# Batch 3's key and value loads issued at other places, and two masks of batch 1 moved, in a block-sparse attention and feed-forward kernel

## The chip, the cores and the metric

The kernel runs on one core of one Trainium2 chip. A core has TensorE (PE, matrix products, with its weight loads shown as PEld), VectorE (DVE), ScalarE (ACT), GpSimd (POOL) and SyncE (SP). POOL and SP also issue the DMAs here: POOL those that read the inputs (queue q0, "software_dynamic" in the profile), SP those between tiles, the transposing ones and the stores of the output (queue q1, "hardware_dynamic"). The metric is the device time of one execution in microseconds; the median of three runs counts.

## The reference, cut to what matters

Attention over 4 batches, 8 heads, 768 positions and 64 channels. A query sees the keys less than 16 positions away, and 24 block summaries: the maximum of the keys and the mean of the values of each block of 32. A feed-forward part follows, with x * sigmoid(1.702 x) between two products (512 to 2048 to 512).

```python
k_sum = k.reshape(B, H, nb, block, D).max(axis=3)
v_sum = v.reshape(B, H, nb, block, D).mean(axis=3)
scores_all = concat([where(|i - j| < 16, scale * q @ k.T, -1e9),
                     scale * q @ k_sum.T + log(block)], axis=-1)
a = softmax(scores_all)
x = a @ concat([v, v_sum])
h = x @ w_in
out = (h * sigmoid(1.702 * h)) @ w_out
```

## The kernel before, in words

The four batches run in a software pipeline: while batch b is in its feed-forward part, the attention of batch b+1 is done beside it. Every engine's instructions are recorded through the helper class `_Ordered`, which keeps the program order on each engine; so nearly every instruction in the profile carries that helper's line, L28, and the order written in the code is the order on the engine. Groups are told apart by their tiles.

One pass of the main loop, `for b in range(0, B - 1)`, has two parts. In the first, a loop over `n` in steps of 2, the first product of the feed-forward of batch b runs (tiles `ph`, 128x384, into `gT` by GELU), and beside it the keys and queries of batch b+1 are prepared. In the second, a loop over the 21 steps of `seq`, the second product runs (`product`, tiles poA, poB, poC), and `beside(b + 1, i)` puts small pieces of the attention of batch b+1 behind step i: the lists `plan1` (batch 1), `plan2` (batch 2) and `plan` (batch 3) say which. In them `sHP` is a group of scores with its exponential (half H, head pair P), `mHP` its mask (`a_sb` times `mk` on DVE), `vHG` the value product of two head pairs (`ps_av`) with its division on DVE (`rc`, `x`), `W0` to `W3` are the four copies of the block sums, `K`, `Q`, `V` issue loads, and `X` starts the transposing DMAs of the keys.

**Tiles.** `kxs[s]` and `qTs[s]` hold transposed keys and queries, `vw[s]` values, of batch b with s = b % 2. `kb` (two buffers) is where keys land before they are transposed by SP (`xk`); `qb` is the same for queries (`xq`). `rest_k(p, s, pool)` completes the keys of head pair p: DVE takes the maxima of the blocks (`ks<-kx`), POOL copies the halos (`kx<-kx`, three copies) and the block maxima (`kx<-ks`, one). For batch 2 it is called at n/2 = 3, 4, 5, 6 of the first part of b = 1, for pairs 0 to 3. The scores of pairs 0 and 1 follow at slot -1 of the second part, those of pairs 2 and 3 at slot 3.

**Block-sum rows.** `value_rows` sums the values of each block on PE (`ps_vs`); `sum_rows` copies the sums, in four groups of two heads, into partitions 0 to 31 of `vw[s]` (`vw<-vboth`; groups 0 and 2 on ACT, 1 and 3 on DVE in batch 2). Behind the last group `sum_dmas` has SP send all of these rows to partitions 64 to 95 of the other half of the tile (`vw<-vw`, 198 KB); the first value product `v00` at slot 10 needs them there.

**Loads of batch 3.** They are issued by POOL in `load_batch(3)`, called behind step 0 of the second part of b = 1. A gate, a copy of one element into `gate2` on POOL, makes POOL wait until the tile that it reads is written:

```python
if b == 3:
    pool.tensor_copy(out=gate2, in_=qTs[0][:, 0, 0:1])
load_turned(k, b, kb2, "kb")          # four loads of keys
if b == 3:
    pool.tensor_copy(out=gate2, in_=qTs[0][:, NP - 1, 0:1])
...
load_v(b)                             # four loads of values
```

The query loads of batch 3 come later, in `middle`, which is the first part of b = 2. At steps 10, 13, 15 and 16 of the second part of b = 1 sums of weights are made for `middle` by `win_sum`, on DVE and POOL (tiles `kx<-w_in_sb` and `qT<-w_in_sb`, in the storage of keys and queries that are done with).

Of the kernel before, what the change touches and what calls it, by code (L numbers as in the profile page):

```python
# [35 lines left out]
def kernel(  # L36
# [10 lines left out]
    B, H, S, D = q.shape  # L47
    block = 32
# [4 lines left out]
    NP = H // 2  # L53
    QT = 64
    NQ = S // QT
    NJ = S // 128
# [10 lines left out]
    pool = _Ordered(tc, nc.gpsimd)  # L67
# [13 lines left out]
    kb2, qb2 = {}, {}  # L81
# [26 lines left out]
    def load_turned(x, b, t2, name, gs_=(0, 1)):  # L108

        for g in gs_:  # L110
            t2[g] = castp2.tile([128, 2, NJ, 2, D], BF16, name=name, tag=name)
            for hh in range(2):
                h0 = hh * NP + 2 * g
                pool.dma_start(out=t2[g][:, :, :, hh].rearrange("p i a d -> p (i a) d"),
                               in_=x[b, h0:h0 + 2].rearrange("h (a p) d -> p (h a) d", p=128))

    def load_v(b):
        src = v[b].rearrange("h (j e p) d -> e p (h j) d", e=2, p=64)
        n = NJ * H // 2
        for i in range(2):  # L120
            for e in range(2):
                pool.dma_start(out=vw[b % 2][e * 64:e * 64 + 64, e].rearrange("p h j c -> p (h j) c")[:, i * n:i * n + n, 0:D],
                               in_=src[e, :, i * n:i * n + n])
# [71 lines left out]
    qTs = [keep.tile([128, NP, S], BF16, name=f"qT{s}") for s in range(2)]  # L195
    qT = [[qTs[s][:, p] for s in range(2)] for p in range(NP)]
    vw = [keep.tile([128, 2, H, NJ, VC], BF16, name=f"vw{s}") for s in range(2)]
# [39 lines left out]

    def load_batch(b):
        if b == 3:
            pool.tensor_copy(out=gate2, in_=qTs[0][:, 0, 0:1])  # L240
        load_turned(k, b, kb2, "kb")
        if b == 3:
            pool.tensor_copy(out=gate2, in_=qTs[0][:, NP - 1, 0:1])
        if b == 1:
            load_turned(q, b, qb2, "qb", (0,))
        load_v(b)
        if b < 3:
            load_turned(q, b, qb2, "qb", (1,) if b == 1 else (0, 1))
# [89 lines left out]
    def at(ap, start, dims):  # L338
        a = ap[:, start:start + 1]
        return bass.AP(tensor=a.tensor, offset=a.offset, ap=[a.ap[0]] + dims)  # L340

    def flat_kx(p, s):
        return kx[p][s].rearrange("p t c -> p (t c)")

    def key_rows(p, s, ks, eng=dve, j0=0):
        flat = flat_kx(p, s)
        n = NJ - j0
        eng.tensor_copy(out=at(flat, 256 * j0 + 64, [[256, n], [64, 2], [1, nb]]),
                        in_=ks.unsqueeze(1).unsqueeze(1).to_broadcast([128, n, 2, nb]))

    def key_halos(p, s, eng=dve, j0=0):

        flat = flat_kx(p, s)
        b0 = max(j0, 1)
        o = 256 * j0
        eng.tensor_copy(out=at(flat, 256 * b0 + 96, [[256, NJ - b0], [1, 16]]),
                        in_=at(flat, 256 * b0 - 16, [[256, NJ - b0], [1, 16]]))
        eng.tensor_copy(out=at(flat, o + 128 + 48, [[256, NJ - 1 - j0], [1, 16]]),
                        in_=at(flat, o + 256, [[256, NJ - 1 - j0], [1, 16]]))
        eng.tensor_copy(out=at(flat, o + 128 + 32, [[256, NJ - j0], [-48, 2], [1, 16]]),  # L360
                        in_=at(flat, o + 48, [[256, NJ - j0], [144, 2], [1, 16]]))
# [211 lines left out]
    def rest_k(p, s, eng=dve):  # L573
        ks = attp.tile([128, nb], BF16, name="ks", tag="ks")
        dve.tensor_reduce(out=ks.rearrange("p (j e n) -> p j e n", e=2, n=2),
                          in_=at(flat_kx(p, s), 0, [[256, NJ], [192, 2], [block, 2], [1, block]]),
                          axis=AX.X, op=ALU.max)
        key_halos(p, s, eng)
        key_rows(p, s, ks, eng)
# [95 lines left out]
    def ff_one(half, nt):  # L675
        ph = pmm.tile([128, HALF], F32, name="ph", tag="mm")
        ff_step(ph, half, nt)
        gelu(half, nt, ph)
# [25 lines left out]
    K1, K2 = slice(0, KO, 2), slice(1, KO, 2)  # L704
# [170 lines left out]
    gate2 = consts.tile([128, 1], BF16, name="gate2")  # L875
# [139 lines left out]
    load_batch(1)  # L1015


    plan1 = {0: ['j0', 't0'], 1: ['j1'], 2: ['t1', 'k3', 'e', 'K0', 'h'], 4: ['s00', 'R', 'W0', 'W1', 'W2', 'W3'], 5: ['j2', 's01', 's10'], 6: ['j3', 'm00', 'm01', 'K1'], 7: ['t2', 's11', 'm10', 'Q0'], 8: ['t3', 'm11', 'Q1', 'V'], 9: ['s02', 's03'], 10: ['m02', 'm03'], 11: ['s12', 's13'], 12: ['g', 'v00', 'v01'], 15: ['x00', 'm12'], 16: ['x01', 'm13', 'X0', 'X1']}
    XE = {}

    plan = {-1: ["s00", "s01"], 2: ["m00", "m01"], 3: ["s02", "s03"], 5: ["m02", "m03", "s10", "s11"],
# [130 lines left out]
    def run1(steps):  # L1152

        for what in steps.split():
            i = int(what[1:])
            if what[0] == "A":
                ff_open(0, order2[0:i], None)
            elif what[0] in "ab":
                ff_one("ab".index(what[0]), order2[i])
            elif what[0] == "v":  # L1160
                values(1, 1, i)
            elif what[0] == "x":
                tx(1, i, act)
            else:
                g_sums(i)
# [23 lines left out]
    def last_pools(stack):  # L1189
        for ab in (True, False):  # L1190
            plast[ab] = stack.enter_context(tc.tile_pool(name=f"plast{ab:d}", bufs=2, space=bass.MemoryType.PSUM,
                                                         reuse_waits="tile"))
# [47 lines left out]
    for b in range(0, B - 1):  # L1240
        nxt = b + 1 < B
        s = (b + 1) % 2
        if b == 1:
            mid.close()
            mid = ExitStack()
            pmm = mid.enter_context(tc.tile_pool(name="pmm", bufs=4, space=bass.MemoryType.PSUM, reuse_waits="tile"))
        if b:
            halves[0] = True
            if b == B - 2:
                mid.close()  # L1250
                mid0.close()
                mid, mid0 = ExitStack(), ExitStack()
                last_pools(mid)
                middle(b, s)
                mid.close()
                mid = ExitStack()
                pmm = mid.enter_context(tc.tile_pool(name="pmm", bufs=4, space=bass.MemoryType.PSUM,
                                                     reuse_waits="tile"))
                psb = mid0.enter_context(tc.tile_pool(name="psb", bufs=2, space=bass.MemoryType.PSUM, side="right",
                                                      reuse_waits="tile"))  # L1260
            for n in range(0, NT if b < B - 2 else 0, 2):
                if b == 1 and n in XB:
                    run1(XB[n])
                elif n == 0:
                    ff_open(0, order2[0:4], None)
                elif n == 2:
                    for nt in order2[0:4]:
                        ff_one(1, nt)
                    g_sums(0)
                    g_sums(1)  # L1270
                else:
                    for nt in order2[n:n + 2]:
                        for half in range(2):
                            ff_one(half, nt)
                        if b == 1 and n + 2 == NT and nt == order2[n]:
                            value_rows(s)
                    g_sums(n // 2, dve, (0, 1) if n + 2 == NT else (0, 1, 2, 3))
                if nxt:
                    if n // 2 in (0, 1):
                        xq(n // 2, s)  # L1280
                    if 3 <= n // 2 < 3 + NP:
                        rest_k(n // 2 - 3, s, pool)
        if nxt:
            if b:
                exp_soon()
            beside(b + 1, -1)
        i = 0
        for t, what in seq if b else seq0:
            product(b, t, what)
            if b < B - 2 and i == (2 if b else 0):  # L1290
                g_sums(NT // 2 - 1, dve, (2, 3))
            for t_, w in OUTG.get(i, ()) if b == 2 else ():
                g_sums(0, dve, (w,), NT // 2, t_, t_ + 1)
            for w, eng in WSUM.get(i, ()) if b == 1 else ():
                if i == 13:
                    pool.tensor_copy(out=gate2, in_=wsi[0][:, 0, 0:1])
                win_sum(w, (dve, pool)[eng])
            if nxt:
                beside(b + 1, i)
            i += 1  # L1300
            if nxt and b + 2 < B:
                if i == 1 and b:
                    load_batch(b + 2)
                if b and i in (16, 18):
                    xk(i // 2 - 8, b % 2)
# [4 lines left out]
    b, n = B - 1, NT // 2  # L1310
# [62 lines left out]
```

## Time and profile before

| What | Value |
|---|---|
| Median of 3 runs (all of them) | 206.83 us (205.57, 207.19, 206.83) |
| The profiled execution: its time, its span from first to last instruction | 207.6 us, 205.8 us |
| Mean granted TensorE clock of that execution | 0.992 |
| DMA q0 (issued by POOL), q1 (issued by SP) | 13.64 MB, 13.03 MB |

Times in the views are microseconds from the first instruction. A row of the timeline gives start, duration, engine, line, operation, the tile written and the tile read, shape, and how many instructions are merged in it; in brackets stands the idle time of the engine before it and what ended it. A row of the waits list gives total, number and longest. A row of a DMA view gives the number of transfers, the size of each and the median time from issue to landing; a DMA's row on its engine shows only the issue. In a row by stretches each engine's busy time stands in the order PE, PEld, DVE, ACT, POOL, then the granted clock, the busy share of the DMA engines and GB/s.

### The profile page before, as it was taken

To read this page: it belongs to the slowest core of one execution; us is meant where nothing else is said; L and a number is where in the kernel's file an instruction comes from. 1 tells how busy PE (TensorE), PEld (TensorE's weight loads), DVE (VectorE), ACT (ScalarE), POOL (GpSimd) and SP (SyncE) were. 2 spreads that over 40 slices of the span, in tenths; PEclk is the share of its full clock that TensorE was granted. 3 is DMA by queue.
4 is the path that set the end of the run, shared out by engine and by line. 5 is a ranking of instruction groups with operands and counts; after the bars stand their busy time and mean duration, and the time that the engine had idled before them with its cause. 6 is when DMAs were issued, how large, how long until landed. Compare 5 with 4: busy or idle time off the path is not lost.

```text
span 205.8 us, 5941 instructions
## 1 busy us (share of the span) xinstructions
PE 196.8 (96%) x2428; PEld 145.4 (71%) x2428; DVE 147.6 (72%) x356; ACT 132.4 (64%) x259; POOL 102.5 (50%) x154
## 2 busy tenths in 40 slices
PE   7979999999998999999997999999999999999993
PEld 7648656856887877555886875566888865578882
DVE  6855785799999544699887874989999436758221
ACT  2382869968898757776981246789770577984220
POOL 7975899358088910056963489240000009991000
PEclk9996999999999999999999999999999999999999
DMA  5999999999999999993999999999122930000222
GB/s 58 160 159 200 197 206 163 191 160 148 128 134 232 192 172 203 118 213 47 68 158 200 163 148 117 139 248 129 24 102 70 179 114 0 0 3 0 102 105 102
DMA packets 98426, 27.03 MB, mean 131 GB/s; under 512 B 87072, under 2 KB 95264, under 8 KB 98400
## 3 DMA queue, kind: packets, MB, share of 16 engines
q0 software_dynamic: 73680, 13.64, 93.8%
q1 hardware_dynamic: 24720, 13.03, 32.2%
q8 instruction: 19, 0.31, 0.6%
q14 instruction: 7, 0.06, 0.1%
HBM read 27.26 MB, written 6.29 MB: 163 GB/s over the span
## 4 chain that ended last, share of the span: by engine, by line
PE 78%; DMA 7%; ACT 5%; DVE 3%; POOL 3%; issue 1%; POOLq 0%; DVEq 0%
PE ph L28 27%; PE poA L28 17%; PE poB L28 8%; PE phA L28 6%; PE ps_av L28 5%; PE poC L28 4%; DMA v0n<-in_v_dram 4%; DMA vw<-vw 3%; ACT a_sb L28 2%; PE phC L28 2%; PE phB L28 2%; PE phE L28 1%; PE ps_s L28 1%; POOL kb L28 1%; PE ps_x L28 1%; ACT L28 1%
## 5 line engine op out<-in xcount | busy, mean ns | idle before, releaser
L28 PE MATMUL ph<-xT,w_in_sb 128*128 128x384 f16 x352 | 62.1, 326 | 0.1
L28 PEld LDWEIGHTS <-w_in_sb 128*128 128x128 f16 x412 | 39.5, 98 | 25.3 <-issue 0.7
L28 ACT ACTIVATE gT<-ph 128x384 f16<-128x384 f32 x88 | 41.8, 492 | 17.5 <-PE ph L28 16.9
L28 PEld LDWEIGHTS <-gT 128*128 128x128 f16 x384 | 36.1, 98 | 5.8 <-issue 0.6
L28 PEld LDWEIGHTS <-gs 128*128 128x128 f16 x288 | 27.7, 98 | 3.4
L28 ACT ACTIVATE a_sb<-ps_s 128x768 bf16<-128x768 f32 (+1 forms) x32 | 24.7, 824 | 5.2 <-PE ps_s L28 5.2
L28 PE MATMUL poA<-ws,gT 128*128 128x256 f16 x192 | 25.0, 273 | 0.7 <-DVE osb L28 0.7
L28 POOL TENSOR_TENSOR gs<-gT 128x384 f16<-128x384 f16 x7 | 6.4, 910 | 28.3 <-ACT gT L28 28.3
L28 POOL DMA_DIRECT2D qb<-in_q_dram x18 | 16.7, 940 | 4.5 <-DMA v0n<-in_v_dram 2.1
L28 POOL COPY kx<-kx 128x80 bf16<-128x80 bf16 (+1 forms) x33 | 11.3, 378 | 15.4 <-DMA kx<-kb 15.4
L28 PEld LDWEIGHTS <-kx 64*128 64x128 bf16 (+1 forms) x396 | 11.7, 95 | 7.7 <-issue 3.9
L28 DVE TENSOR_TENSOR a_sb<-a_sb,mk 128x768 bf16<-128x768 bf16 x28 | 14.4, 551 | 2.6 <-ACT a_sb L28 2.4
L28 DVE TENSOR_TENSOR x<-ps_av,rc 128x768 f16<-128x768 f32 (+1 forms) x20 | 15.8, 796 | 0.6
L28 POOL DMA_DIRECT2D kb<-in_k_dram x16 | 15.3, 976 | 0.9 <-POOLq L1357 0.8
L28 ACT ACTIVATE s<-poA 128x256 f32<-128x256 f32 x17 | 6.5, 385 | 14.1 <-PE poA L28 13.8
L28 ACT ACTIVATE osb<-poA 128x256 f32<-128x256 f32 x12 | 4.6, 384 | 16.4 <-PE poA L28 16.2
L28 POOL COPY kx<-ks 128x288 bf16<-128x288 bf16 x11 | 4.9, 446 | 18.6 <-DVE ks L28 18.6
L28 POOL DMA_DIRECT2D vw<-in_v_dram x12 | 11.5, 978 | 4.2 <-DMA w_out_sb<-in_moe_w_out_dram 3.4
L28 ACT ACT_TABLE_LOAD x10 | 12.8, 1283 | 1.0 <-PEq L1357 0.8
L28 DVE TENSOR_TENSOR gs<-gT 128x384 f16<-128x384 f16 (+3 forms) x19 | 8.6, 450 | 5.8 <-ACT gT L28 5.6
L28 PE MATMUL poA<-w_out_sb,gT 128*128 128x256 f16 x96 | 12.5, 273 | 0.0
L28 PE MATMUL poB<-ws,gs 128*128 128x256 f16 x96 | 12.5, 273 | 0.0
(117 smaller groups left out, 358.1 us busy)
## 6 DMA issues: line engine op xcount, KB each, us to landing
out_dram<-osb SPq DMA_DIRECT2D x23, 256.0 KB, 2.7
kb<-in_k_dram POOLq DMA_DIRECT2D x16, 192.0 KB, 5.9
qb<-in_q_dram POOLq DMA_DIRECT2D x14, 192.0 KB, 8.7
vw<-in_v_dram POOLq DMA_DIRECT2D x12, 192.0 KB, 10.6
w_out_sb<-in_moe_w_out_dram POOLq DMA_DIRECT2D x3, 512.0 KB, 10.4
w_in_sb<-in_moe_w_in_dram POOLq DMA_DIRECT2D x4, 256.0 KB, 9.4
w_in_sb<-in_moe_w_in_dram POOLq DMA_DIRECT2D x2, 512.0 KB, 11.8
v0n<-in_v_dram POOLq DMA_DIRECT2D x4, 192.0 KB, 8.2
```

The costliest lines, as they stand in the source:

```text
L28: r = f(*a, **kw)
```

## The change

Batch 3's key loads leave `load_batch`. The two loads of head pairs 0 and 1 (g = 0) are issued behind `rest_k` of pair 1 in the first part of b = 1, those of pairs 2 and 3 (g = 1) behind `rest_k` of pair 2, each behind a gate copy of its own that reads the query tile of batch 2 (pair 0, pair 3). `load_batch(3)` is called behind step 2 instead of step 0 and issues only the values, behind a gate that reads an element of the last group of block-sum rows of batch 2. In `plan1` the masks m10 and m11 go from slots 7 and 8 to the end of slots 9 and 10, which on DVE puts the two output additions (`osb`) ahead of them. POOL has one gate copy more, and its loads keep their order among themselves; the order on PE, ACT and SP is the same.

```diff
     def load_batch(b):
         if b == 3:
-            pool.tensor_copy(out=gate2, in_=qTs[0][:, 0, 0:1])
-        load_turned(k, b, kb2, "kb")
-        if b == 3:
-            pool.tensor_copy(out=gate2, in_=qTs[0][:, NP - 1, 0:1])
+            pool.tensor_copy(out=gate2[0:block], in_=vw[0][0:block, 1, H - 1, NJ - 1, 0:1])
+        else:
+            load_turned(k, b, kb2, "kb")
         if b == 1:
             load_turned(q, b, qb2, "qb", (0,))
         load_v(b)
...
-    plan1 = {... 7: ['t2', 's11', 'm10', 'Q0'], 8: ['t3', 'm11', 'Q1', 'V'], 9: ['s02', 's03'], 10: ['m02', 'm03'], ...}
+    plan1 = {... 7: ['t2', 's11', 'Q0'], 8: ['t3', 'Q1', 'V'], 9: ['s02', 's03', 'm10'], 10: ['m02', 'm03', 'm11'], ...}
...
                     if 3 <= n // 2 < 3 + NP:
                         rest_k(n // 2 - 3, s, pool)
+                        g = {1: 0, 2: 1}.get(n // 2 - 3)
+                        if b == 1 and g is not None:
+                            pool.tensor_copy(out=gate2, in_=qTs[0][:, g * (NP - 1), 0:1])
+                            load_turned(k, 3, kb2, "kb", (g,))
...
             if nxt and b + 2 < B:
-                if i == 1 and b:
+                if i == 3 and b:
                     load_batch(b + 2)
```

More of the change, by code (lines that the diff above doesn't have):

```diff
@@ L1015 @@
     load_batch(1)
-    plan1 = {0: ['j0', 't0'], 1: ['j1'], 2: ['t1', 'k3', 'e', 'K0', 'h'], 4: ['s00', 'R', 'W0', 'W1', 'W2', 'W3'], 5: ['j2', 's01', 's10'], 6: ['j3', 'm00', 'm01', 'K1'], 7: ['t2', 's11', 'm10', 'Q0'], 8: ['t3', 'm11', 'Q1', 'V'], 9: ['s02', 's03'], 10: ['m02', 'm03'], 11: ['s12', 's13'], 12: ['g', 'v00', 'v01'], 15: ['x00', 'm12'], 16: ['x01', 'm13', 'X0', 'X1']}
+    plan1 = {0: ['j0', 't0'], 1: ['j1'], 2: ['t1', 'k3', 'e', 'K0', 'h'], 4: ['s00', 'R', 'W0', 'W1', 'W2', 'W3'], 5: ['j2', 's01', 's10'], 6: ['j3', 'm00', 'm01', 'K1'], 7: ['t2', 's11', 'Q0'], 8: ['t3', 'Q1', 'V'], 9: ['s02', 's03', 'm10'], 10: ['m02', 'm03', 'm11'], 11: ['s12', 's13'], 12: ['g', 'v00', 'v01'], 15: ['x00', 'm12'], 16: ['x01', 'm13', 'X0', 'X1']}
     XE = {}
```

## The prediction

> **What bounds the kernel now.** I read the page's busy shares first, then the list of what TensorE (PE) waited for, then the timeline around each of its waits, then the DMA view of the same stretches.
>
> ```profile
> span 205.8 us, 5941 instructions
> PE 196.8 (96%) x2428; PEld 145.4 (71%) x2428; DVE 147.6 (72%) x356; ACT 132.4 (64%) x259; POOL 102.5 (50%) x154
> ```
> ```profile
> engine line waited for: us in total, times, longest us
> ...
> PE ps_av L28 <- DMA vw<-vw: 1.4, 1, 1.4
> ...
> PE poA L28 <- DVE osb L28: 0.7, 1, 0.7
> ```
>
> PE is busy for 96% of the span, so only what makes PE wait can be won. Two of its waits lie where the change works: 1.4 us for a copy of value rows inside the tile vw, and 0.7 us for VectorE (DVE) to add an output tile. The first:
>
> ```profile
> 100.60 0.86 DVE L28 COPY vw<-vboth 32x768 bf16<-32x768 bf16 x1
> 101.79 0.52 PE L28 MATMUL ps_s<-qT,kx 64*128 64x64 bf16 x24
> ...
> 103.40 0.35 DVE L28 COPY vw<-vboth 32x768 bf16<-32x768 bf16 x1
> ...
> 108.62 1.04 PE L28 MATMUL poC<-w_out_sb,gT 128*128 128x256 f16 x8
> ...
> 110.04 1.22 DVE L28 TENSOR_TENSOR kx<-w_in_sb 128x2048 f16<-128x2048 f16 x1
> ...
> 111.08 0.96 PE L28 MATMUL ps_av<-vw,a_sb 128*64 128x65 bf16 x48 [1.42 <-DMA vw<-vw]
> ...
> 111.69 0.23 DVE L28 RECIPROCAL rc<-ps_av 128x12 f32<-128x12 f32 x1 [0.43 <-PE ps_av L28]
> 111.95 0.96 DVE L28 TENSOR_TENSOR x<-ps_av,rc 128x768 f16<-128x768 f32 x1
> ...
> 113.08 0.96 DVE L28 TENSOR_TENSOR x<-ps_av,rc 128x768 f16<-128x768 f32 x1
> ...
> 114.69 0.95 PE L28 MATMUL ps_av<-vw,a_sb 128*64 128x65 bf16 x48
> ```
>
> DVE's last block-sum copy (W3) ends at 103.75, and SyncE (SP) then sends the rows on to other partitions. PE is through with its products at 109.66 and stands until 111.08. What the rows met, from the DMA view of 103.8 to 107, and the same transfer of batch 1 and of batch 3 in their own stretches:
>
> ```profile
> q0 software_dynamic: 3862, 0.49, 239.8%
> ...
> vw<-vw SPq DMA_DIRECT2D x1, 198.0 KB, 7.1
> ```
> ```profile
> vw<-vw SPq DMA_DIRECT2D x1, 198.0 KB, 4.6
> ```
> ```profile
> vw<-vw SPq DMA_DIRECT2D x1, 198.0 KB, 2.6
> ```
>
> For 3.2 us after the issue every packet (3862) is of q0, the queue that POOL fills with the key and value loads of batch 3, and none is SP's. The same 198 KB took 2.6 us in batch 3 and 4.6 us in batch 1, so 7.1 us is mostly waiting behind POOL's loads.
>
> The Trainium skill ("DMA: Bandwidth & Descriptors", Queues, rings and completion order) says that each DMA engine takes turns between its queues packet by packet. By that rule SP's rows would not stand for 3.2 us without one packet; the trace differs here, and the measurement decides.
>
> **The change part by part.**
>
> *Key loads earlier.* POOL's order around them before, with the stretches in which their data starts:
>
> ```profile
> 93.23 1.11 POOL L28 COPY kx<-kx 128x80 bf16<-128x80 bf16 x3
> 95.06 0.43 POOL L28 COPY kx<-ks 128x288 bf16<-128x288 bf16 x1 [0.72 <-DVE ks L28]
> 95.43 1.19 POOL L28 COPY kx<-kx 128x80 bf16<-128x80 bf16 x3
> 97.75 0.43 POOL L28 COPY kx<-ks 128x288 bf16<-128x288 bf16 x1 [1.13 <-DVE ks L28]
> 98.12 0.19 POOL L28 COPY gate<-qT 128x1 bf16<-128x1 bf16 x1
> 98.24 4.06 POOL L28 DMA_DIRECT2D kb<-in_k_dram  x4
> ...
> 102.44 3.81 POOL L28 DMA_DIRECT2D vw<-in_v_dram  x4
> ```
> ```profile
> 99.00:100.00 1.00, 1.00 (x12) 0.90 (x10) 0.54 (x2) 0.99 (x3) 1.00 (x2) 1.00 0.01 1
> 100.00:101.00 1.00, 1.00 (x12) 0.90 (x10) 0.82 (x2) 1.00 (x2) 1.00 (x2) 1.00 1.63 105
> ```
> ```profile
> kb<-in_k_dram POOLq DMA_DIRECT2D x1, 192.0 KB, 4.3
> ```
> ```profile
> 84.51 5.28 SPq L28 DMA_TRANSPOSE qT<-qb  x2
> ```
> ```profile
> qT<-qb SPq DMA_TRANSPOSE x1, 5.7
> ```
> ```profile
> qT<-qb SPq DMA_TRANSPOSE x1, 3.8
> ```
>
> A gate copy (0.19) and two loads (half of 4.06, 2.03) go ahead of the key halos of head pair 2, the same again ahead of pair 3. Worked along POOL in before's clock: gate and loads 93.23 to 95.45, halos to 96.56, rows of pair 2 to 96.99 (its maxima were ready at 95.06), gate and loads to 99.21, halos of pair 3 to 100.40, rows to 100.83. Before, pair 3 was done at 98.18. The 4.44 us put in cost only 2.65, because POOL had idled 0.72 and 1.13 before its rows. PE reads pairs 2 and 3 at 101.79: 1.0 us of cover, 0.5 if PE has come forward by 0.48 (below) and POOL has not. I take a cost of 0; with no idle time absorbed, pair 3 would be ready at 98.18 + 4.44 = 102.62 and PE would wait 0.8, the upper end. The gates wait for nothing: the first query transpose, issued at 84.51, lands 5.7 later at 90.2, the second, issued by 89.79, lands 3.8 later, by 93.6 at the latest, against gates at 93.2 and 97.0. The second pair of loads finds an idle queue: the first load of before landed 4.3 us after its issue, so issues at 97.2 and 98.2 land by about 101.5 and 103.2 (estimate: the second 0.7 us slower than the first behind it). Both are down before the rows leave at 103.8.
>
> *Value loads behind the rows.* The new gate reads what W3 writes, so POOL and SP are released together at 103.75. The gate takes 0.2. Data of a POOL load starts nearly 2 us after its issue (issue 98.24, 1 GB/s until 100, 105 after), so the first value packet comes at about 105.8. The rows alone need 2.6 us (landing 106.4), with POOL traffic beside them 4.6 (108.4); PE asks for them at 109.66. Either way the wait goes: 1.42 us. The lower end is 0, if the rows again take over 7 us; anything under 5.8 us gives all of it, and both other rows are under that, so I take 1.42. The loads end their issue at about 107.8 instead of 106.25 and nothing of POOL's is queued behind them until 111. Their consumer is far:
>
> ```profile
> vw<-in_v_dram POOLq DMA_DIRECT2D x1, 192.0 KB, 10.3
> ```
> ```profile
> 124.39 0.31 PE L28 MATMUL ps_vs<-vw,E 64*32 64x128 bf16 x16
> ```
>
> The last load, issued at about 106.8, would land at 117 even after the same 10.3 us; PE wants it at 122.5 after the shift.
>
> *What is late next.* DVE's weight sum at 110.04 to 111.26 lay in PE's wait. With the first value product at 109.66 its reciprocal must wait for that sum: it starts 0.43 earlier, not 1.42. The second x then ends at 113.6 instead of 114.04, and the next value products (114.69 moved to 113.27, their second half at 113.75) need its PSUM bank. 0.15 us of cover is left: no cost, but nearly one.
>
> *Two masks later.* Batch 0's tail:
>
> ```profile
> 64.20 1.48 DVE L28 TENSOR_TENSOR a_sb<-a_sb,mk 128x768 bf16<-128x768 bf16 x3
> ...
> 65.17 4.05 POOL L28 DMA_DIRECT2D qb<-in_q_dram  x4
> ...
> 65.60 0.41 DVE L28 TENSOR_TENSOR osb<-poA,s 128x256 f32<-128x256 f32 x1
> ...
> 66.07 1.03 PE L28 MATMUL poA<-ws,gT 128*128 128x256 f16 x8 [0.66 <-DVE osb L28]
> ...
> 66.74 1.01 DVE L28 TENSOR_TENSOR a_sb<-a_sb,mk 128x768 bf16<-128x768 bf16 x2
> ...
> 69.34 1.09 PE L28 MATMUL ps_av<-vw,a_sb 128*64 128x65 bf16 x48
> ```
>
> The third of the three masks no longer stands before the output add that PE waits for: the add starts 1.48/3 = 0.49 earlier and PE with it; 0.48 of its 0.66 us go (bounds 0 and 0.66). The moved masks run where DVE idles, and the two masks that the value product needs at 69.34 stay ahead of the second of them, done by about 67.5. Between here and 109 the list names no wait of PE, so the 0.48 reaches the rows' stretch, where everything moves with it.
>
> **The sum.** 1.42 + 0.48 = 1.90 us. The profiled execution took 207.6 us with a span of 205.8; it would take 205.7 with 203.9. It lies 0.8 above the median of the runs, 206.83 (205.57 to 207.19); from that median the forecast is 204.9 us, 0.9% faster. A measurement of this kernel can tell about 1% from no change, so this sits just inside that line.
>
> **The rivals.**
> 1. *DVE takes the place of the rows.* If DVE slips by more than the 0.15 us of cover, PE is tied to it and wins only DVE's own 0.43 there: 206.83 - 0.48 - 0.43 = 205.9. For it: DVE is nearly back to back from 109.7 on. Against it: the cover is there by the rows.
> 2. *The rows stay late.* The value loads start only 0.2 us behind the rows' issue; if SP's packets are again held, only the masks count: 206.35. Against it: the rows have some 2 us without rivals, and alone they need 2.6. By the skill's turn-taking rule named above POOL's queue would not be what held the rows, and clearing it would win nothing there either; 3862 packets to none speak against that.
> 3. *Batch 2's keys come late, and it is slower.* PE pays when pair 3 ends after 101.8, that is when the four issues take more than 0.25 us longer each than 1.02; it eats the whole gain at about 0.7 us each. At double length they add 4.1 us: 3.1 us of wait, 206.83 - 1.9 + 3.1 = 208.0. For it: POOL's issues now stand beside a busy DVE, and W1's DVE copy took 0.86 us beside POOL's loads where W3 took 0.35. Against it: the query loads at 65.17 ran beside DVE's masks at 1.01 us each. The Trainium skill ("SBUF — State Buffer", the "DVE blocks DMA" trap) says that a DVE copy in its two-port mode locks GpSimd out while it would write descriptors, 620 ns becoming 3100; by that factor it would be some 15 us slower. No row here shows it.
>
> **How the numbers follow.** Both waits go 0.60 (204.9, its own range 204.3 to 205.6), DVE in its place 0.16 (205.9), rows late 0.14 (206.35), keys late 0.10 (208.0). The range 204.2 to 206.6 leaves out the slow case and the tails. Below 204.76 (over 1% faster) lies some 45% of the first case: 0.28. Over 208.9 lies the worse part of the last: 0.06. The rest, 0.66, is within 1%.
>
> **What would show it.** In the changed profile: no wait of PE for vw<-vw, the rows of batch 2 landing in under 5 us, q1 packets within 2 us of their issue; POOL's rows of pair 3 done before the scores of slot 3, with no PE wait for POOL; the wait for osb at 0.2 us or less; reciprocals right behind the weight sum. A PE wait for kx, or for x behind the value products, would make the forecast wrong, as would POOL issues over 1.3 us each.

## The result, and the profile after

The changed kernel took 204.5 us (median of 22 runs, 204.15 to 206.64), the kernel before, run beside it, 206.58 us (22 runs, 205.57 to 208.64). The ratio is 0.9918, with a 95% interval from 0.9894 to 0.9943: about 1.7 us, or 0.8%, faster. That is the ratio of the means; the medians lie 2.1 us apart, because the changed kernel's runs stand in two groups, fifteen at 204.15 to 204.91 us and seven at 205.3 to 206.64. Forecast were 204.9 us and 1.90 us.

From the page of the changed kernel, the span and the busy times:

```profile
span 204.3 us, 5944 instructions
...
PE 196.3 (96%) x2428; PEld 144.5 (71%) x2428; DVE 146.8 (72%) x356; ACT 132.4 (65%) x259; POOL 102.0 (50%) x155
```

The engines do the same work for as long as before; what went is idle time of PE. What PE waited for (total, number of times, longest):

```profile
engine line waited for: us in total, times, longest us
PE ps_q L28 <- DMA qb<-in_q_dram: 1.5, 1, 1.5
...
PE ps_vs L28 <- DMA vw<-in_v_dram: 0.3, 1, 0.3
...
PE poA L28 <- DVE osb L28: 0.2, 1, 0.2
```

The wait for `vw<-vw` (1.4) is gone from the list, and that for `osb` has fallen from 0.7 to 0.2. The largest entry now, 1.5 us for a query load, belongs to the start-up, which the change doesn't touch. Such waits for loads differ from execution to execution. The 0.3 us for the values of batch 1 (`ps_vs`) is another of them; the list of the kernel before has no such entry, and this is most of why the pair of spans, 205.8 and 204.3, differs by 1.5 us only.

The timeline of the changed kernel around the rows, with POOL's, DVE's and PE's instructions:

```profile
93.17 0.31 POOL L28 COPY gate<-qT 128x1 bf16<-128x1 bf16 x1
93.42 2.04 POOL L28 DMA_DIRECT2D kb<-in_k_dram  x2
...
97.03 2.03 POOL L28 DMA_DIRECT2D kb<-in_k_dram  x2
...
99.72 0.43 POOL L28 COPY kx<-ks 128x288 bf16<-128x288 bf16 x1
100.54 0.35 DVE L28 COPY vw<-vboth 32x768 bf16<-32x768 bf16 x1
...
101.73 0.52 PE L28 MATMUL ps_s<-qT,kx 64*128 64x64 bf16 x24
...
103.48 0.18 POOL L28 COPY gate<-vw 32x1 bf16<-32x1 bf16 x1 [3.33 <-DVE vw L28]
104.03 3.81 POOL L28 DMA_DIRECT2D vw<-in_v_dram  x4 [0.37 <-issue]
...
108.56 1.04 PE L28 MATMUL poC<-w_out_sb,gT 128*128 128x256 f16 x8
109.53 0.96 PE L28 MATMUL ps_av<-vw,a_sb 128*64 128x65 bf16 x48
...
109.98 1.21 DVE L28 TENSOR_TENSOR kx<-w_in_sb 128x2048 f16<-128x2048 f16 x1
111.11 0.22 DVE L28 RECIPROCAL rc<-ps_av 128x12 f32<-128x12 f32 x1
...
112.50 0.96 DVE L28 TENSOR_TENSOR x<-ps_av,rc 128x768 f16<-128x768 f32 x1
113.14 0.95 PE L28 MATMUL ps_av<-vw,a_sb 128*64 128x65 bf16 x48
```

The value product at 109.53 follows the product at 108.56 without a bracket, where before it stood 1.42 us. Behind it on DVE, after an output add, stand the weight sum and only then the reciprocal, as forecast. And the DMA view of the same kernel in the first microsecond behind SP's issue of the rows, 103.4 to 104.4:

```profile
DMA packets 0, 0.00 MB, mean 0 GB/s; under 512 B 0, under 2 KB 0, under 8 KB 0
...
vw<-vw SPq DMA_DIRECT2D x1, 198.0 KB, 4.0
```

Where before this stretch was full of POOL's packets, there is nothing: the key loads are down and the value loads have not begun. The rows landed in 4.0 us instead of 7.1. Batch 0's tail, in the timeline of the changed kernel:

```profile
64.61 1.01 DVE L28 TENSOR_TENSOR a_sb<-a_sb,mk 128x768 bf16<-128x768 bf16 x2
...
65.54 0.41 DVE L28 TENSOR_TENSOR osb<-poA,s 128x256 f32<-128x256 f32 x1
...
66.01 1.03 PE L28 MATMUL poA<-ws,gT 128*128 128x256 f16 x8 [0.16 <-DVE osb L28]
66.21 2.08 DVE L28 TENSOR_TENSOR a_sb<-a_sb,mk 128x768 bf16<-128x768 bf16 x4
```

Two masks stand ahead of the output add instead of three, and PE's wait is 0.16 instead of 0.66 us. The place itself lies at almost the same time as before (66.01 and 66.07), because PE reached it some 0.4 us later: shortly before, it had stood for batch 1's values, where before it had not.

```profile
58.74 0.56 PE L28 MATMUL ps_vs<-vw,E 64*32 64x128 bf16 x43 [0.35 <-DMA vw<-in_v_dram]
```

So the fall from 0.66 to 0.16 is not the masks' work alone (more on this under the experiments). From the output add's product to the value product it is 43.52 us (66.01 to 109.53), and before 45.01 (66.07 to 111.08): 1.49 less, of which the rows' wait is 1.42.

### The profile page after: what moved, and what is told of

Same layout as the page of the kernel before. It is cut to its first block, busy times and chain, and to the rows that moved or that the text cites. A ratio compares the mean times of both kernels' runs of the same rounds, so it can differ in the third digit from the quotient of the medians.

```text
span 204.3 us, 5944 instructions
## 1 busy us (share of the span) xinstructions
PE 196.3 (96%) x2428; PEld 144.5 (71%) x2428; DVE 146.8 (72%) x356; ACT 132.4 (65%) x259; POOL 102.0 (50%) x155
## 4 chain that ended last, share of the span: by engine, by line
PE 66%; DMA 17%; POOL 10%; DVE 3%; issue 2%; ACT 0%; POOLq 0%; DVEq 0%
PE ph L28 18%; PE poA L28 18%; PE poB L28 9%; DMA kb<-in_k_dram 7%; PE phA L28 6%; DMA vw<-in_v_dram 6%; DMA w_in_sb<-in_moe_w_in_dram 5%; PE poC L28 4%; POOL mk L28 3%; PE ps_av L28 3%; PE ps_s L28 2%; POOL v0n L28 2%; POOL w_out_sb L28 2%; PE phC L28 2%; PE phB L28 2%
## 5 line engine op out<-in xcount | busy, mean ns | idle before, releaser
L28 POOL COPY kx<-kx 128x80 bf16<-128x80 bf16 (+1 forms) x33 | 10.3, 352 | 13.8 <-DMA kx<-kb 13.7
L28 PE MATMUL poC<-w_out_sb,gT 128*128 128x256 f16 x96 | 12.5, 273 | 0.2 <-ACT gT L28 0.2
```

What stands on the lines that cost most here:

```text
L28: r = f(*a, **kw)
```

## The experiments

The question was which of the three parts brings the time, and by which mechanism. The theory on record: the rows were late because of POOL's loads ahead of them, keys and values both, so both had to move; the masks add 0.48 us. The rivals: DVE takes the place of the rows; the queue order does not matter; the early keys cost something.

| Run | Ratio to before, 95% interval | Rows landed in, us | PE's waits at the two places, us |
|---|---|---|---|
| before | 1 | 7.1 | rows 1.4, osb 0.7 |
| changed kernel | 0.9918 (0.9894 to 0.9943) | 4.0 | osb 0.2 |
| the same again (e5) | 0.9912 (0.9874 to 0.9950) | 4.1 | none |
| masks alone (e1) | 0.9956 (0.9924 to 0.9989) | 7.0 | rows 1.3 |
| loads alone (e2) | 0.9912 (0.9879 to 0.9946) | 4.5 | osb 0.6 |
| keys alone (e3) | 0.9988 (0.9962 to 1.0015) | 6.5 | rows 0.7 |
| values alone (e4) | 0.9919 (0.9890 to 0.9948) | 4.6 | osb 0.7 |
| values and masks (e6) | 0.9898 (0.9840 to 0.9957) | 4.6 | osb 0.3 |
| the same again (e12) | 0.9950 (0.9915 to 0.9984) | 4.7 | none |
| values and three masks (e11) | 0.9916 (0.9888 to 0.9945) | 4.5 | none |

The `osb` entries depend on something else as well, as keys alone shows: it leaves the masks at their old slots, and `osb` is off its list all the same. In that profile, and then in that of masks alone, PE had stood for the values of batch 1 some 7 us earlier:

```profile
57.88 0.56 PE L28 MATMUL ps_vs<-vw,E 64*32 64x128 bf16 x43 [0.93 <-DMA vw<-in_v_dram]
```
```profile
57.88 0.56 PE L28 MATMUL ps_vs<-vw,E 64*32 64x128 bf16 x43 [0.67 <-DMA vw<-in_v_dram]
```

This wait changes between executions, from none to 0.93 us over all the profiles, and nothing in the change touches it. Where PE has stood there, DVE's output add comes in time for it or makes it wait less. In the profiles whose list has no such entry, the wait for `osb` is 0.61 to 0.74 us with the masks at their old slots (before, loads alone, values alone) and 0.22 to 0.32 us with the two moved (values and masks, and the run with the gate on W1 below). So the moved masks take away some 0.4 us in executions in which batch 1's values are in time; where PE has stood for them, less is left to take away.

### Masks alone, loads alone

The first is the kernel before with the changed `plan1`; the second the changed kernel with the old one:

```diff
-    plan1 = {... 7: ['t2', 's11', 'm10', 'Q0'], 8: ['t3', 'm11', 'Q1', 'V'], 9: ['s02', 's03'], 10: ['m02', 'm03'], ...}
+    plan1 = {... 7: ['t2', 's11', 'Q0'], 8: ['t3', 'Q1', 'V'], 9: ['s02', 's03', 'm10'], 10: ['m02', 'm03', 'm11'], ...}
```

> The kernel before with the two masks moved and the loads left where they were. Theory A (PE is the bound, the two waits add): PE's wait for osb falls from 0.7 us to 0.2 or less, the wait for the rows stays at about 1.4 us, the time falls by 0.48 us (ratio 0.9977). Rival (the time won in batch 0 is given back at the next fixed point, the landing of the rows): the wait for osb falls and the wait for the rows grows by as much, ratio 1.000.

> The change without the two masks. Theory A: the wait for the rows goes, the wait for osb stays at 0.7 us, the time falls by 1.42 us (ratio 0.9931), and this with the masks alone adds up to the whole. Rival (DVE takes the place of the rows): only DVE's own 0.43 us are won, ratio 0.998, and PE waits for x behind the value products.

Masks alone took 205.76 us (12 runs) against 207.04 (29). Its list of waits keeps the rows and has no entry for `osb` (which, with the 0.67 us for batch 1's values ahead of it, does not show what the masks do):

```profile
PE ps_av L28 <- DMA vw<-vw: 1.3, 1, 1.3
```

Loads alone took 204.98 us (6 runs) against the same 207.04, and its list has no entry for the rows and keeps `osb`:

```profile
PE poA L28 <- DVE osb L28: 0.6, 1, 0.6
```

So the loads take away the rows' wait and leave that for `osb`, and the masks leave the rows' wait. What the masks are worth the times leave open: alone they gain 0.1 to 0.8%, but on top of the loads nothing shows (0.9912 for the loads alone; 0.9918 and 0.9912 for the whole change). The intervals, 0.3% to either side, are wider than the 0.23% that 0.48 us would be.

### Keys alone, values alone

Keys alone is loads alone with the values back behind step 0, where nothing holds them:

```diff
-            pool.tensor_copy(out=gate2[0:block], in_=vw[0][0:block, 1, H - 1, NJ - 1, 0:1])
+            pool.tensor_copy(out=gate2, in_=qTs[0][:, NP - 1, 0:1])
...
-                if i == 3 and b:
+                if i == 1 and b:
                     load_batch(b + 2)
```

Values alone is loads alone with the keys back behind step 0:

```diff
-                        g = {1: 0, 2: 1}.get(n // 2 - 3)
-                        if b == 1 and g is not None:
-                            pool.tensor_copy(out=gate2, in_=qTs[0][:, g * (NP - 1), 0:1])
-                            load_turned(k, 3, kb2, "kb", (g,))
...
+                if i == 1 and b:
+                    pool.tensor_copy(out=gate2, in_=qTs[0][:, 0, 0:1])
+                    load_turned(k, 3, kb2, "kb")
                 if i == 3 and b:
                     load_batch(b + 2)
```

> The key loads moved as in the change, the value loads left behind step 0 without waiting for the rows, the masks left. Theory A (rows wait for what POOL's queue holds when they are issued): four loads instead of eight stand around the rows, all issued by 102.1, their data through at about 106 (four of 192 KB at about 130 KB per us from 100 on); the rows' first packet comes at about 106, they land at about 107.5 to 108.5, 4 to 5 us after their issue, PE does not wait, and the time falls by 1.4 us (ratio 0.993). Rival B (what counts is the value traffic beside the rows): the wait stays, ratio 1.000.

> The value loads behind the rows as in the change, the key loads left behind step 0, the masks left. Theory A (rows wait for what POOL's queue holds when they are issued): the four key loads, issued from 98.2 to 102.3 and landing until 107.4 before, still stand ahead; the rows' first packet comes at about 106 to 107, they land at 109.5 to 111, 6 to 7 us after their issue, and at most 0.6 us of the 1.42 is won (ratio 0.997 to 1.000). Rival B (what counts is the value traffic beside the rows): the rows land in under 5 us and the whole 1.42 us is won (ratio 0.993).

In both runs the theory on record missed, and its rival, that the value loads are what counts, came nearer. Keys alone gave 206.96 us (12 runs), no difference that can be measured; half of the rows' wait stays. Its waits, and its DMA view from the rows' issue at 102.76 on, 102.8 to 105.2:

```profile
PE ps_av L28 <- DMA vw<-vw: 0.7, 1, 0.7
```
```profile
q0 software_dynamic: 2587, 0.33, 213.9%
...
vw<-vw SPq DMA_DIRECT2D x1, 198.0 KB, 6.5
```

With the keys out of the way, the value loads run into the same place: for 2.4 us after the issue every packet is again of q0, POOL's queue. Values alone gave 205.11 us (12 runs), all that the loads bring. Its DMA view from 102.9 to 104.5 (the rows were issued at 102.97), and then from 104.6 to 107.6:

```profile
q0 software_dynamic: 1908, 0.24, 237.1%
...
vw<-vw SPq DMA_DIRECT2D x1, 198.0 KB, 4.6
```
```profile
q0 software_dynamic: 1529, 0.19, 103.6%
q1 hardware_dynamic: 192, 0.47, 52.9%
```

Here the key loads are still under way when the rows leave, and for 1.5 us the rows get nothing. Then both queues run side by side, and 4.6 us is early enough: PE asks for the rows 5.8 us after their issue. So the value loads behind the rows bring the time by themselves. In the prediction the early keys were needed to have the queue empty; they aren't.

### How much POOL traffic ahead is too much

The changed kernel, with the value loads' gate on the second group of the rows (W1) instead of the last, so that they are issued from 101.26 on, two to three of the four ahead of the rows:

```diff
-            pool.tensor_copy(out=gate2[0:block], in_=vw[0][0:block, 1, H - 1, NJ - 1, 0:1])
+            pool.tensor_copy(out=gate2[0:block], in_=vw[0][0:block, 1, 3, NJ - 1, 0:1])
```

> The changed kernel with the value loads' gate on the second of the four groups of block-sum rows instead of the last, so that the four value loads are issued some 2.4 us earlier, at about 101 to 105 us, around the rows' issue at 103.4; the key loads are already down. If traffic of POOL's that was issued ahead of the rows holds them, and only as much as it is, one to two loads stand ahead: the rows' first packets come 1.5 to 2.5 us after their issue (3.2 before, 1.0 in the changed kernel), they land in 5 to 6.5 us (7.1 and 4.0), and PE waits 0 to 0.5 us for vw<-vw. If the queues simply take turns, the place of the issue does not matter while the loads overlap the rows: landing as in the changed kernel, 4 to 4.6 us, and no wait. If it is all or nothing, 7 us and 1.0 to 1.4 us of wait.

It was executed once (205.97 us), so only its profile is read. Its DMA view from 103.4, where the rows were issued, to 105.3:

```profile
q0 software_dynamic: 1927, 0.24, 201.6%
...
vw<-vw SPq DMA_DIRECT2D x1, 198.0 KB, 5.7
```

1.9 us without a packet of SP's, landing after 5.7 us at 109.1, and no wait of PE for the rows, which it asked for at 109.26. That is the first of the three expectations: the more POOL has issued ahead of the rows, the later they land. In order of POOL's traffic ahead, over all the profiles:

| POOL's loads still under way when the rows are issued | Rows landed in, us |
|---|---|
| hardly any (four profiles: the changed kernel twice, loads alone, the doubled sum below) | 3.7 to 4.5 |
| the rest of the keys (five: values alone, and those with two or three masks on top) | 4.5 to 5.2 |
| two to three value loads (this run) | 5.7 |
| three to four value loads (keys alone) | 6.5 |
| the second pair of keys and two to three value loads (the values ahead of everything, below) | 6.7 |
| keys and values (before, masks alone) | 7.1, 7.0 |

The first two ranges meet, so what the keys cost is small; the values cost some 2 us. Not all of the time without a packet is holding: in the changed kernel, with both queues empty, the first 1.0 us passes without one too. The limit lies at the 5.8 us after which PE asks.

### The values ahead of everything

The changed kernel with the four value loads right behind the second pair of key loads, with no gate, so that they would be down before the rows leave:

```diff
                             load_turned(k, 3, kb2, "kb", (g,))
+                            if g == 1:
+                                load_v(3)
...
-                if i == 3 and b:
-                    load_batch(b + 2)
```

> The changed kernel with the value loads issued right behind the second pair of key loads, so ahead of pair 3's halos on POOL, and with no gate. My rival of late keys, made to happen: POOL's rows of pair 3 end 3.8 us later, at 103.5 to 104.5 where PE asks at 101.7; PE waits about 2.2 us for kx, the rows of block sums go out later too and hide their own wait, and the time is 206.6 - 1.9 + 2.2, ratio 1.001 (0.998 to 1.004). Rival (POOL's order has no hold on PE here): no wait for POOL and a ratio of 0.992.

It took 209.73 us (4 runs), 1.0133 of before (1.0067 to 1.0199): slower, and by more than expected, since PE waited 4.4 us instead of 2.2. The timeline of POOL, and PE's scores of pair 3:

```profile
94.41 0.36 POOL L28 COPY gate<-qT 128x1 bf16<-128x1 bf16 x1 [2.28 <-DMA qT<-qb]
...
100.42 3.81 POOL L28 DMA_DIRECT2D vw<-in_v_dram  x4
...
104.86 0.46 POOL L28 COPY kx<-ks 128x288 bf16<-128x288 bf16 x1
...
105.38 0.50 PE L28 MATMUL ps_s<-qT,kx 64*128 64x64 bf16 x12 [4.39 <-POOL kx L28]
```

Two things show here. The four issues stand for 3.81 us ahead of the key halos in POOL's order. In the changed kernel pair 3 was ready 1.58 us before PE asked for it (100.15 and 101.73), so for these issues alone PE would wait the expected 2.2 us. And the first gate of the early keys stood 2.28 us for the transpose of the queries, which the prediction had excluded ("the gates wait for nothing"); with it, 3.81 + 2.28 - 1.58 is 4.5, and PE waited 4.39. That transpose, issued by SP at 83.78 here and at 84.31 in the changed kernel, landed late in both; the DMA view of the changed kernel, and then that of this one:

```profile
qT<-qb SPq DMA_TRANSPOSE x1, 8.4
```
```profile
qT<-qb SPq DMA_TRANSPOSE x1, 10.6
```

Before it was 5.7 us. All three kernels are the same up to there, so this is a spread between executions; over all fourteen profiles it runs from 5.7 to 10.6 us. In the changed kernel it landed at 92.7, with 0.4 us to the gate at 93.17, which shows no wait; here it landed at 94.4. With such a wait, and without the value loads' 3.81, pair 3 would have been done at 105.32 - 3.81 = 101.5, against 101.0 (105.38 - 4.39), where PE asked for it: half a microsecond lost, by this estimate. So the third rival is a real edge of the early keys. Of the seven profiles with early keys this is the one in which the gate waits; how often the gate waits in executions without a profile can't be seen here.

### DVE's cover behind the rows

The changed kernel with the weight sum at step 10 done twice on DVE, which delays the reciprocals by 1.2 us:

```diff
+                if w == 0:
+                    win_sum(w, dve)
```

> The changed kernel with the first weight sum on DVE, which stands ahead of the value products' reciprocals, done twice (1.2 us more on DVE, with the same result). If the cover behind the rows is as small as worked out (0.15 us): the second x ends 1.2 us later, PE waits 0.9 to 1.1 us at the next value products or the product behind them, and the time is 0.9 to 1.1 us above the changed kernel, ratio to before 0.996 (0.994 to 0.998). Rival (DVE has room there): no wait, ratio 0.991.

It took 206.01 us (12 runs), 0.9976 of before (0.9941 to 1.0011). Its waits:

```profile
PE ps_av L28 <- DVE x L28: 1.0, 2, 0.6
```

1.21 us more on DVE became 1.0 us of PE's waiting at once, so the cover there is 0.2 us (0.15 was worked out). The prediction's first rival was that close; it did not come about because nothing on DVE slipped.

### The version without the early keys, and one step further

"Values and masks" is values alone with the changed `plan1`; the changed kernel was run again beside it.

> The changed kernel once more, as the yardstick for the three beside it. Theory A: no wait for the rows, at most 0.2 us for osb, ratio to the kernel before 0.991 (0.989 to 0.994). Rival (the masks add nothing, since the loads alone gave 0.9912): the same number as the loads alone, 0.991; the two cannot be told apart by this run alone, only by the wait for osb in the profile.

> Value loads behind the rows and the two masks moved; key loads left behind step 0. If moving the keys adds nothing (as the values alone suggest, 0.9919): the rows land in 4.3 to 5 us, PE does not wait for them, and the ratio is that of the whole change, 0.991 (0.989 to 0.994). If the keys are needed beside it: a wait for the rows of 0.3 us or more, and a ratio of 0.993 or above.

205.51 us (12 runs, changed kernel) and 204.84 (6 runs) against 206.52 (23): the early keys bring nothing that shows. Then two moves on top: m01 from slot 6 to slot 9, and the first weight sum one step later, behind the x's of slot 10:

```diff
-    plan1 = {... 6: ['j3', 'm00', 'm01', 'K1'], ... 9: ['s02', 's03', 'm10'], ...}
+    plan1 = {... 6: ['j3', 'm00', 'K1'], ... 9: ['s02', 's03', 'm01', 'm10'], ...}
...
-    WSUM = {10: [(0, 0)], 13: [(2, 1)], 15: [(1, 0)], 16: [(3, 1)]}
+    WSUM = {11: [(0, 0)], 13: [(2, 1)], 15: [(1, 0)], 16: [(3, 1)]}
```

> This is the version with the keys at their old place, the values behind the rows and the two later masks, with two more moves: m01 goes from slot 6 to slot 9, and the first weight sum from slot 10 to slot 11, so that DVE does it behind the second x of slot 10 and not ahead of the first. If the small rest of the wait for the output add and DVE's sum behind the rows are what is left to win there, PE's wait for osb (0.2 to 0.3 us in the changed kernel and in its version without the key move) is gone from the list and the reciprocal starts right behind the first value products, with no wait of PE for x; the time is then 0.2 to 0.3 us under the version without these two moves, about 0.989 of the kernel before. The rival, that both are already covered, gives 0.990 as before and a list of waits that is no shorter; and if the sum at its new place stands before something of slot 13, PE waits there for DVE by up to 1.2 us and the ratio is 0.995.

It took 205.78 us (12 runs) against 206.75 (17), 0.9965 (0.9929 to 1.0000): near the last of the three expectations, with half of the gain lost. From its timeline:

```profile
111.94 1.21 DVE L28 TENSOR_TENSOR kx<-w_in_sb 128x2048 f16<-128x2048 f16 x1
...
113.45 4.07 POOL L28 TENSOR_TENSOR kx<-w_in_sb 128x2048 f16<-128x2048 f16 x1
...
115.67 2.93 DVE L28 TENSOR_TENSOR kx<-kx,w_in_sb 128x2048 f16<-128x2048 f16 x1
...
119.31 1.03 PE L28 MATMUL poA<-ws,gT 128*128 128x256 f16 x8 [0.68 <-DVE osb L28]
```

POOL's sum waits for DVE's first one and so starts 4.7 us behind the first value product (113.45 and 108.73), where it was 2.0 us in the changed kernel (111.48 and 109.53). DVE's second sum at 115.67 now falls beside it and takes 2.93 us instead of 1.2; the output adds behind it are late and PE stands 0.68 us. Without the sum's move, and with the two-mask version again beside it:

> Keys at their old place, values behind the rows, and three masks of batch 1 moved later instead of two (m01 too, from slot 6 to the start of slot 9), with the first weight sum back at slot 10. What remained of PE's wait for the output add in batch 0's tail, 0.2 to 0.3 us, should go, as it went in the run with the sum moved, and no wait of PE for osb at 115 to 120 should come, since POOL's sums again stand clear of DVE's: DVE's second sum takes 1.2 us again, where it took 2.9 us beside POOL's. Expected 0.988 to 0.990 of the kernel before, 0.2 to 0.3 us under the kernel with two masks moved. The rival, that not the moved sum but the third mask cost what was lost there, gives 0.995 again.

> The kernel with the values behind the rows and two masks later, once more, on the same chip as the one with three masks: 0.990 to 0.992 of the kernel before if the key move is worth nothing; a wait of PE for osb of 0.2 to 0.3 us in batch 0's tail. If the early keys do bring something after all, 0.995.

Three masks: 204.95 us (11 runs, 203.77 to 205.78), two masks: 205.77 (12 runs, 204.12 to 207.02), both against 206.65 (22 runs). With three masks the wait for `osb` is off the list, and the second sum is back at its length:

```profile
115.67 1.22 DVE L28 TENSOR_TENSOR kx<-kx,w_in_sb 128x2048 f16<-128x2048 f16 x1
```

So the 0.68 us of waiting came with the moved sum and not with the third mask. For the two-mask version e12 (0.9950) came out at the value that its expectation gave to the case that early keys bring something, where e6, the same kernel, had 0.9898. The intervals overlap (0.9915 to 0.9957), and so do those of the changed kernel: a value of the early keys of up to some 0.4% is neither shown nor excluded by the times. No wait that they take away shows in the profiles. None of the versions is shown to beat the changed kernel; three masks, with the lowest single time, is 0.9916.

## Why the prediction was right, and where it was not

*The rows' wait, 1.42 us:* right, in size and place. PE waits 0 for them, and the next value products start at 113.14 where 113.27 was worked out. The bounds, 2.6 us for the rows alone and 4.6 beside traffic, held: 4.0. The mechanism, POOL's loads ahead of SP's transfer, is shown by moving them: the more was issued ahead, the later the rows landed.

*Two masks, 0.48 us:* right in kind, and somewhat less in size. The pair of profiles gives 0.66 to 0.16, but there batch 1's values came late in the second; with the values in time it is from 0.61 to 0.74 down to 0.22 to 0.32, some 0.4 us, and where PE has already stood for the values there is less or nothing to win. The prediction took the 0.66 of one profile for a fixed wait. By the times masks alone is faster by 0.1 to 0.8%, which holds 0.48 us (0.23%) and does not measure it.

*The early keys, cost 0:* the price held. Pair 3 was done at 100.15, where 100.83 was worked out, well ahead of the scores at 101.73. The reason given for having them failed: the values alone clear the rows. They were also down with less to spare than worked out: the first load of the second pair, issued at 97.03, took 5.6 us and not 4.3, and the second was down at about 103.4, just as the rows were issued. The step "the gates wait for nothing" failed as well, as the run with the values ahead shows; it took the landing of one transpose from one profile, 5.7 us, for a fixed time, and that landing ranged up to 10.6 us, against 3 us of margin at the first gate.

*DVE late next:* right. The reciprocal starts at 111.11 behind the sum, the second x ends at 113.46 (113.6), and the next value products don't wait. The cover of 0.15 us was confirmed by using it up.

*The rivals.* The rows that stay late: by the rule that the Trainium skill gives ("DMA: Bandwidth & Descriptors", Queues, rings and completion order), that each engine takes turns between its queues by packets, clearing POOL's queue would have won nothing. In four kernels (before, keys alone, the gate on W1, values alone) SP's transfer got no packet for 1.5 to 3.2 us while POOL's queue ran, against some 1.1 us with both queues empty, so the rule does not describe the start; once the rows were under way, the two queues did run side by side (192 packets to 1529 in values alone), which the rule allows, though these counts don't show turns. What holds the start, no run here tells. The late keys came true in another kernel only, through four more issues and a waiting gate, and not through slower issues: two took 2.04 us, as before.

*The sum:* 1.90 us forecast, 1.7 measured (1.2 to 2.2 by the interval). That the two lie so close is in part luck: of the two terms only the rows' is secured, and by the times the loads alone gain as much as the whole change.

## What to carry to other kernels

A transfer that an engine waits for should be looked at with everything that other queues have issued shortly before it, and a cheap remedy is to put the non-urgent loads behind it with a gate on what releases it; here those loads had 7 us to spare (the last landed at about 115.5, and PE read them at 122.85). When two things stand ahead of a late transfer, it is enough to remove as much as brings it under its due time: work out that time first (5.8 us here) and move the part that nothing waits for, here the values. A wait that one profile shows can be smaller or absent in the next execution, as that for `osb` was, so its worth should be read from several. A gate that waits for nothing in one profile is only free if its margin is larger than the spread of what it reads.

## What the runs showed of the hardware beyond that

DVE stood behind POOL on a sum from tile to tile. In the run with the sum moved, DVE's 128x2048 sum took 2.93 us beside POOL's of 4.07, against 1.22 alone, and ended 1.08 us after POOL's (118.60 and 117.52): almost its own length, as if it had stood until POOL was through. The Trainium skill ("SBUF — State Buffer", SBUF: two separate sides) states it so for a DVE instruction with both inputs in SBUF, as here, beside a POOL instruction that reads SBUF: the port pair that the two share is an exclusive lock, and the one that comes second blocks fully. The trace agrees.

The DVE copy of 32x768 values that took 0.86 us before, beside POOL's key loads, took 0.35 in the changed kernel with POOL idle (100.54). In values alone the loads stand beside it again:

```profile
99.41 2.04 POOL L28 DMA_DIRECT2D kb<-in_k_dram  x2
99.76 0.86 DVE L28 COPY vw<-vboth 32x768 bf16<-32x768 bf16 x1
```

So here it was DVE that paid for POOL's issues; POOL's issues themselves took 1.02 us each in either place. It is not so every time: before's other copy took 0.35 us at 103.40, in the middle of POOL's value issues (102.44 to 106.25), so the contrast that the prediction's third rival drew between the two was none, and in keys alone the copies beside the value issues took 0.35 (at 99.67) and 0.58 (at 102.12). What decides it, no run here shows.
